# First loads on two queues, a reordered opening, and joined stores of tail rows in a fused attention and MLP kernel

## The chip, the cores and the metric

The kernel runs on one core of a Trainium2 chip. The time is the device time of one execution in microseconds (us). The core has a matrix engine (PE, with its weight loads PEld), a vector engine (DVE), a scalar engine (ACT), a general engine (POOL) and a queue engine (SP). SP, ACT and POOL can issue transfers ("SPq", "ACTq", "POOLq" in the profile); a column "DMA share" gives the mean busy share of the core's 16 transfer engines.

An execution over 1.5% above the fastest of the same kernel is marked slow and left out of the comparisons. The runs were made on several chips; each kernel is compared with the kernel before in the same rounds on the same chip. A profile is of one execution.

## The reference

```python
# attention: q, k, v of (8 batches, 8 heads, 576 tokens, 64), a band of 32 tokens to each side
scores = np.matmul(q, k.transpose(0, 1, 3, 2)) / np.sqrt(D)
scores = np.where(np.abs(pos[:, None] - pos[None, :]) <= 32, scores, -1e9)
x = softmax(scores) @ v                      # then (8 * 576, 512): tokens by heads and d
# MLP
h = x @ w_in                                 # 512 x 2048
g = 0.5 * h * (1 + np.tanh(c * (h + 0.044715 * h**3)))
out = g @ w_out                              # 2048 x 512
```

## The kernel before

The 4608 tokens are worked through in nine tiles of 512. While PE computes the MLP of tile t, the attention of batch t + 1 is slipped between its matmuls, by a fixed plan. In the opening, batch 0 has nothing to hide behind; `spin` issues matmuls without use, meant to keep PE's clock up. Queries are stored so that token 4p + j lies at (j, p), and the last 24 (in batch 0: 16) positions p, the "tail rows", are handled apart.

```python
def load_early(b):                      # opening: batches 0 and 1, all on SP
    def qk(h0):
        for src, dst in ((q, qr), (k, kr)):
            nc.sync.dma_start(dst[:, h0:h0 + 2, :], src[b, h0:h0 + 2, 0:512, :]...)
...
def load_v(b):                          # later batches: four casting loads on POOL, and the tail
    for c in range(4):
        nc.gpsimd.dma_start(V[:, c, :, :], v[b, :, 128 * c:128 * c + 128, :]...)
...
def cast_and_turn(b):                   # later batches: casts on DVE, transposes by transfers on SP
    ...
    nc.sync.dma_start_transpose(QTs[b]..., dst...)
    ...
            nc.sync.dma_start_transpose(KTs[b % 2]..., k16...)
...
def store(t, t4, yo, cols=slice(0, 512), eng=None):      # 128 rows of results
    m = 0
    while m < 128:
        ...                             # b, j, p of row m; n positions p to a j in this part
        e = min(n - p, 128 - m)
        ...
        (... nc.gpsimd).dma_start(out_v[b, j, q0 + p:q0 + p + e, cols], yo[m:m + e, cols])
        m += e
```

In the middle of the kernel POOL does, for each tile: eleven stores, then four V loads of a later batch. SP issues the transposes of the next batch's queries and keys (QT, KT).

The softmax here doesn't subtract the row's maximum and nothing guards it: scores larger than these inputs give would overflow.

## Time and profile before

| | before |
|---|---|
| median of the first 3 runs | 304.15 us (302.09 to 307.22) |
| span of the profiled run | 302.4 us, PE busy 96% |
| first product (x times w_in) starts | 21.03 us |
| second product (times w_out) starts | 40.86 us |
| from the first score of one middle batch to the next | 30.4 us |
| last result on DVE ready | 297.92 us |

The prediction shows the lines behind most of it. Three things that became important are not in it. The first is the transposes of a middle batch on SP's queue (start, length of the issue), which are issued in the first stretch of each tile:

```profile
94.67 3.44 SPq L324 DMA_TRANSPOSE QT<-q  x1
98.20 5.85 SPq L331 DMA_TRANSPOSE KT<-k  x2
```

The second is what POOL issues at that time: the stores of a tile, and right behind them the V loads.

```profile
91.75 7.10 POOL L515 DMA_DIRECT2D out_dram<-y  x11 [14.40 <-DVE y L580]
98.83 3.62 POOL L175 DMA_DIRECT2D V<-in_v_dram  x4
```

The first V load is issued 98.83 - 94.67 = 4.2 us after the QT transpose. The third is PE at the scores that need the transposes (start, length, what; idle time before and its cause would stand in brackets):

```profile
106.65 0.62 PE L360 MATMUL ps_s<-QT,KT 64*64 64x96 f16 x32
107.66 1.48 PE L551 MATMUL mm<-w_out,gT 128*128 128x256 f16 x12
...
110.92 0.40 PE L360 MATMUL ps_s<-QT,KT 64*64 64x96 f16 x16
```

No bracket: PE does not wait. The scores at 106.65 (head pairs 0 and 1) need the first of the two KT transposes, those at 110.92 (pair 2) the second. No view prints when these landed, but the trace holds the semaphore events: the first had landed at 105.68, so 1.0 us was to spare, and the second at 110.18. At batches 3 to 6 the spare time before the first scores was 1.0, 1.6, 3.6 and 1.6 us. The page did not show how little that was, since a wait that does not happen leaves no line.

### The profile page before, as it was taken

The numbers are of one execution on the slowest core, as the hardware profiler recorded it, in microseconds if no ns is written. First come the engines' busy times: TensorE is split into PE (matmuls) and PEld (weight loads), VectorE is DVE, ScalarE is ACT, GpSimd is POOL, SyncE is SP. The second block draws the span as 40 slices with busy tenths as digits, with TensorE's granted clock in tenths as the row PEclk, the third lists the DMA queues.
The fourth block names the chain that finished last, engine by engine and source line by source line (L and its number), as shares of the span: only waits on it lengthen the run. The fifth ranks groups of instructions, "written<-read, shape, count | busy, mean of one in ns | idle before, by whom it ended". The sixth has DMA issues, their size and how long they took to land.

```text
span 302.4 us, 7135 instructions
## 1 busy us (share of the span) xinstructions
PE 289.4 (96%) x2886; PEld 181.3 (60%) x2886; DVE 195.0 (64%) x429; ACT 186.9 (62%) x287; POOL 104.6 (35%) x160
## 2 busy tenths in 40 slices
PE   6869999999999999999999999999999999999993
PEld 2434545444785488547854785478547864784582
DVE  4682679969969566956685668566866635442442
ACT  1555767487856695669566956785668666606500
POOL 3555546357008500850085007600710070015000
PEclk9997999999999999999999999999999999999999
DMA  6989999999998999899979995999690031004013
GB/s 187 249 270 386 363 332 246 242 271 186 207 211 167 171 214 193 191 152 230 201 166 181 234 197 136 168 239 194 101 212 11 2 92 49 3 15 124 2 46 94
DMA packets 116831, 52.44 MB, mean 173 GB/s; under 512 B 97519, under 2 KB 109551, under 8 KB 116798
## 3 DMA queue, kind: packets, MB, share of 16 engines
q1 hardware_dynamic: 84233, 39.66, 59.7%
q0 software_dynamic: 31776, 11.41, 33.0%
q10 hardware_dynamic: 789, 0.92, 0.9%
q8 instruction: 22, 0.36, 0.5%
q14 instruction: 11, 0.09, 0.1%
HBM read 36.70 MB, written 9.44 MB: 153 GB/s over the span
## 4 chain that ended last, share of the span: by engine, by line
PE 71%; DMA 11%; SPq 8%; DVE 5%; POOL 2%; issue 2%; ACT 0%; DVEq 0%; POOLq 0%
PE mm L551 31%; PE mm L456 18%; PE ph L456 14%; DMA wst<-in_moe_w_in_dram 4%; DMA wst<-in_moe_w_out_dram 3%; SPq L145 3%; PE ps_s L360 2%; PE ps_d L389 2%; DMA kr<-in_k_dram 2%; DMA vr<-in_v_dram 2%; SPq L136 2%; DVE s L499 2%; PE ps_o L395 2%; SPq L167 2%; POOL w_in L201 1%
## 5 line engine op out<-in xcount | busy, mean ns | idle before, releaser
L456 PEld LDWEIGHTS <-w_in 128*128 128x128 f16 x576 | 56.4, 99 | 68.3 <-issue 2.4
L515 POOL DMA_DIRECT2D out_dram<-y x77 | 46.4, 611 | 113.0 <-DVE y L580 99.3
L456 PE MATMUL mm<-xT,w_in 128*128 128x512 f16 x320 | 79.3, 382 | 1.7 <-POOL w_in L201 1.7
L464 ACT ACTIVATE gT<-mm 128x512 f16<-128x512 f32 x80 | 47.6, 599 | 46.0 <-PE mm L456 45.2
L456 PE MATMUL ph<-xT,w_in 128*128 128x512 f16 x256 | 65.0, 383 | 0.0
L499 DVE TENSOR_TENSOR s<-gT 128x512 f16<-128x512 f16 x64 | 26.9, 420 | 41.7 <-ACT gT L464 41.7
L551 PEld LDWEIGHTS <-s 128*128 128x128 f16 x512 | 49.6, 98 | 5.9
L551 PE MATMUL mm<-t,s 128*128 128x256 f16 x376 | 44.7, 273 | 0.0
L370 ACT ACTIVATE pe<-ps_s 128x960 f16<-128x960 f32 (+1 forms) x32 | 30.5, 976 | 22.5 <-PE ps_s L360 22.4
L464 ACT ACTIVATE gT<-ph 128x512 f16<-128x512 f32 x64 | 36.0, 602 | 10.1 <-PE ph L456 9.9
L551 PEld LDWEIGHTS <-gT 128*128 128x128 f16 x384 | 36.0, 98 | 6.6
L551 PE MATMUL mm<-w_out,gT 128*128 128x256 f16 x256 | 32.8, 273 | 0.5 <-DVE y L562 0.5
L409 ACT ACTIVATE lt<-lt 128x480 f32<-128x480 f32 (+3 forms) x40 | 23.5, 587 | 1.3
L408 ACT ACTIVATE lt<-ps_d 128x480 f32<-128x480 f32 (+2 forms) x29 | 16.0, 553 | 11.1 <-PE ps_d L389 6.2
L175 POOL DMA_DIRECT2D V<-in_v_dram x24 | 22.0, 938 | 1.7 <-PE mm L456 1.3
L90 ACT ACT_TABLE_LOAD x17 | 21.8, 1283 | 1.1 <-PEq L812 0.8
L376 DVE TENSOR_TENSOR pe<-pe,band 128x960 f16<-128x960 f16 (+1 forms) x32 | 21.3, 684 | 1.0 <-ACT pe L370 1.0
L395 PEld LDWEIGHTS <-V 128*64 128x64 f16 x520 | 14.5, 111 | 4.0 <-DVE V L183 0.6
L551 PE MATMUL mm<-t,gT 128*128 128x256 f16 x128 | 16.3, 273 | 0.0
L418 DVE TENSOR_TENSOR xT<-ps_o,lt 128x480 f16<-128x480 f32 (+5 forms) x26 | 13.4, 535 | 2.0 <-ACT lt L409 1.9
L360 PEld LDWEIGHTS <-KT 64*64 64x64 f16 x576 | 9.6, 106 | 8.1 <-issue 5.8
L551 PE MATMUL mm<-w_out,s 128*128 128x256 f16 x120 | 14.4, 273 | 0.0
(90 smaller groups left out, 305.2 us busy)
## 6 DMA issues: line engine op xcount, KB each, us to landing
kr<-in_k_dram SPq DMA_DIRECT2D x32, 256.0 KB, 8.4
qr<-in_q_dram SPq DMA_DIRECT2D x6, 1024.0 KB, 7.8
wst<-in_moe_w_in_dram SPq DMA_DIRECT2D x3, 1024.0 KB
wst<-in_moe_w_out_dram SPq DMA_DIRECT2D x3, 1024.0 KB, 11.9
V<-in_v_dram POOLq DMA_DIRECT2D x24, 128.0 KB, 7.9
qr<-in_q_dram SPq DMA_DIRECT2D x8, 256.0 KB, 10.5
vr<-in_v_dram SPq DMA_DIRECT2D x16, 128.0 KB, 3.4
V<-V SPq DMA_DIRECT2D x5, 256.0 KB
```

Source lines behind the costliest of these rows:

```text
L90: nc.scalar.add_instruction(mybir.InstLoadActFuncSet(name=nc.get_next_instruction_name(), act_func_set_id=which, ins=[], outs=[]))
L175: nc.gpsimd.dma_start(V[:, c, :, :], v[b, :, 128 * c:128 * c + 128, :].rearrange("h p d -> p h d"))
L370: nc.scalar.activation(pe, ps[:, :, 0:w], AF.Exp, scale=SCALE)
L376: nc.vector.tensor_tensor(pe, pe, m.rearrange("k (o j) p -> k o j p", o=1).broadcast_to(list(pe.shape)), op=ALU.mult)
L395: nc.tensor.matmul(o[64 * h:64 * h + 64, cols].rearrange("d (j p) -> d j p", j=4)[:, :, p0 - q0:p1 - q0], Vs[b % 2][:, slot, 2 * pr + h, : ...
L408: nc.scalar.activation(lt[:, 0:n], d[:, 0:n], AF.Ln)
L409: nc.scalar.activation(lt[:, 0:n], lt[:, 0:n], AF.Exp, scale=-1.0)
L456: nc.tensor.matmul(ph, w_in16[:, dc, fc * 128:fc * 128 + 128], xT[:, dc, t * 512 % RING:t * 512 % RING + 512], start=(dc == 0), stop=(dc = ...
L464: nc.scalar.activation(gTs[t][:, fc, :], phs[fc], AF.Gelu_apprx_tanh)
L499: nc.vector.tensor_tensor(dst, x, y, op=op)
L515: (eng or turn_about[0] if t == NT - 1 else eng or nc.gpsimd).dma_start(out_v[b, j, q0 + p:q0 + p + e, cols], yo[m:m + e, cols])
L551: nc.tensor.matmul(pys["apart"][:, 0:256] if apart else py[:, blk, :], lhsT, wino[w][:, f, :], start=(new and i % (8 if one else 16) == 0) ...
```

## The change

It means to start the opening sooner: the first loads go out on two queues (SP and ACT), the ACT table load moves behind ACT's issues, w_in comes in halves, the attention of batch 0 is ordered anew with some copies on ACT and casts on DVE, and the first product runs chunk by chunk behind it. Besides, the stores of tail rows are joined: several blocks of j, each of 16 or 24 rows, in one transfer; and the last tile's stores are divided between SP and ACT in another way.

```diff
-            for src, dst in ((q, qr), (k, kr)):
-                nc.sync.dma_start(
+            for src, dst, eng in ((q, qr, nc.sync), (k, kr, nc.sync if b else nc.scalar)):
+                eng.dma_start(
...
+                eng = nc.scalar if not b and h in (1, 3) else nc.sync
...
-    load_table(exp_set)          (at the start)
+    load_table(exp_set)          (behind the first loads)
+    for i in range(4):
+        wi.append(load_w_in(i, stage_w(), 0, 2))
+        load_w_in(i, wi[i], 2, 4)
...
+            nj = 1 if p else max(1, min(4 - j, (128 - m) // n))
+            eng = engs[i % len(engs)] if engs else nc.gpsimd
+            if nj > 1:
+                e = nj * n
+                eng.dma_start(out_v[b, j:j + nj, q0:q0 + n, cols], yo[m:m + e, cols])
...                               (the opening: turns, casts, masks and weightings in a new order)
+    spread(0, 2, *ods[2])
+    spin(3, 512, 0)
+    for dc in range(3):
+        for fc in range(4):
+            ffn_in(0, fc, dc, dc + 1)
```

## The prediction

> **What bounds the kernel now.** I read the page first, then the matrix engine in order of time, then the waits, and last the transfers in short stretches. From the page (busy share of PE in 40 slices of 7.56 us, its granted clock, GB/s moved):
> ```profile
> PE 289.4 (96%) x2886; PEld 181.3 (60%) x2886; DVE 195.0 (64%) x429; ACT 186.9 (62%) x287; POOL 104.6 (35%) x160
> PE   6869999999999999999999999999999999999993
> PEclk9997999999999999999999999999999999999999
> ```
> PE is busy 96% of the span. It is not full in the first slices, in the last one, and in the fourth slice its clock falls. A change that removes no product work, as this one, can only gain there: at the opening and at the end. Much of the "busy" time of the opening is filler matmuls (spin). The matrix engine in order of time (start, length, what, idle time before):
> ```profile
> 21.03 0.39 PE L456 MATMUL mm<-xT,w_in 128*128 128x512 f16 x1 [1.52 <-POOL w_in L201]
> 21.59 0.39 PE L456 MATMUL mm<-xT,w_in 128*128 128x512 f16 x1 [0.17 <-POOL w_in L201]
> ...
> 40.86 0.38 PE L525 MATMUL mm<-w_out,gT 128*128 128x512 f16 x1 [0.29 <-POOL w_out L201]
> 41.61 1.67 PE L525 MATMUL mm<-w_out,gT 128*128 128x512 f16 x7 [0.37 <-POOL w_out L201]
> ```
> Twice PE waits for a weight cast: at the first product (21.03 us) and at the second product (40.86 us). From there on the idle times I could find are 0.33 us at 51.6, 0.41 at 60.4 and 0.54 at 79.8; 100 to 280 us is full. So the end moves by what the 40.86 point moves. What do the casts wait for? The waits of 20 to 60 us (total, times, longest):
> ```profile
> POOL w_in L201 <- DMA wst<-in_moe_w_in_dram: 6.6, 5, 1.9
> POOL w_out L201 <- DMA wst<-in_moe_w_out_dram: 6.2, 4, 2.9
> DVE w_in L201 <- DMA wst<-in_moe_w_in_dram: 5.7, 2, 4.1
> ```
> They wait for transfers, not for an engine. Until the second product starts, the kernel is bound by how soon the loads arrive. Short stretches of the opening (columns: busy us of PE, PEld, DVE, ACT, POOL; clock, DMA share, GB/s):
> ```profile
> 2.50:5.00 2.50, 2.50 (x10) 1.11 (x8) 1.34 (x7) 0.00 (x0) 0.50 (x2) 1.00 0.89 268
> ...
> 12.50:15.00 2.50, 2.18 (x41) 0.90 (x39) 2.46 (x5) 1.92 (x3) 1.74 (x3) 1.00 1.23 227
> 15.00:16.25 1.25, 1.25 (x22) 0.80 (x16) 1.16 (x3) 0.90 (x2) 0.69 (x2) 1.00 0.95 199
> 16.25:17.50 1.25, 1.00 (x22) 0.41 (x20) 1.22 (x3) 0.21 (x1) 0.63 (x2) 1.00 0.34 59
> ...
> 20.00:22.50 2.50, 1.30 (x21) 0.66 (x21) 1.67 (x4) 0.75 (x2) 1.90 (x4) 1.00 1.03 368
> 22.50:25.00 2.50, 2.50 (x12) 0.87 (x7) 0.69 (x1) 2.37 (x3) 0.76 (x2) 0.50 1.05 405
> ```
> Two things: a hole of 59 GB/s at 16.25 to 17.50, between the last values and the first weights, and PE at clock 0.50 in 22.5 to 25. The hole stands behind the one issuing queue:
> ```profile
> 7.29 2.05 SPq L136 DMA_DIRECT2D qr<-in_q_dram  x1
> ...
> 10.03 4.70 SPq L145 DMA_DIRECT2D vr<-in_v_dram  x6
> 14.77 3.97 SPq L192 DMA_DIRECT2D wst<-in_moe_w_in_dram  x5
> ```
> An undisturbed issue takes about 0.47 us; the twelfth took 2.05, and the first of w_in 1.57 (14.77 to 16.34). So the queue was held back, the weights were issued late, and the hole followed.
>
> **What the Trainium skill says.** "DMA: Bandwidth & Descriptors", section Issuing engines are not separate DMA queues, says that transfers issued from several engines run on the same 16 DMA engines and that this saves only the issuing time. The DMA share of 0.89 to 1.23 outside the hole agrees: there is little idle engine time to win. The same page, Why small descriptors are slow (HBM only), says that 256-byte rows lose part of the rate. The trace agrees: 199 to 227 GB/s while the values (64 floats, 256 B a row) come, 368 to 405 with weights. "TensorE: Matmul & The Clock Gate", Part 1, says that PE runs at half clock after about 3.4 us without work. Here the fall to 0.50 came after stretches with gaps of at most 1.52 us, so gaps shorter than that page's window count too. "ScalarE: Activation LUTs", What ACT_TABLE_LOAD costs, gives about 1283 ns; the trace shows 1283.
>
> **The change part by part.**
> *Two queues.* Seven of the opening loads (four k, the k tail, values of heads 1 and 3) move from SP to ACT. Batch 0 is q, k and v of 8x576x64 floats each, 3.54 MB; they are in at about 17.5 us (the stretches up to there sum to 3.6 MB). I see three gains. (a) The hole filled at 368 GB/s: (368-59)/368 x 1.25 = 1.05 us. (b) The slice 3.75 to 5.00 moves 162 GB/s, since the tails' issues take 0.62 to 0.75 us for 128 KB each; at the 301 of the next slice that is 174 KB more, 0.47 us at 368. (c) 10 to 16.25 us moves about 225 GB/s; if two queues raised it to the 277 of 5 to 7.5, 325 KB, 0.9 us; I count half, 0.45, for the share there is already over 1. Sum 2.0 us (estimate): all later loads of the queue come 2.0 us sooner.
> *Table load behind the issues.* Seven issues at about 0.6 us end near 5 us, the table load of 1.28 near 6.3; ACT's first work, a copy of QT, was ready on DVE at 5.72. Up to 0.6 us later for the first pair, not on the path: later pairs wait for data.
> *Weights in halves.* w_in 1 arrives whole at 24.7; in halves its first 512 KB (1.4 us at 368) is usable 1.4 us sooner. Casts split DVE/POOL: 0.43 us on DVE against 0.61 on POOL.
> *Attention reordered, product by chunk.* DVE takes two q casts (0.43 each), ACT two QT copies. The last group's weighting no longer stands behind the first two products (it ended at 22.5, though the last value cast ended at 18.4). With values in at about 16, weighting ends near 18, its two ACT steps (0.60 + 0.63) and the multiply (0.69) near 19.6. w_in 0 comes at 18.3 and 19.8, POOL casts by 21.0, PE starts at about 19 and runs 12 products. w_in 1 lands at 22.7: 14 more products, so the seventh column starts at about 25.2, against 28.9 before. PE is then 3.7 us earlier, data only 2.0. Spare PE speed is lost again in waits: w_in 2 (28.45 before) at 26.5, batch 1's k and q (32.7 to 36.5) at 30.7 to 34.5, w_out 0 (39.9) at 37.9. So the second product starts at about 38.9, not 40.86: **2.0 us**. This includes the cold clock: the eight slow products at 0.43 instead of 0.216 us cost 1.7, but w_out 0 would have been waited for anyway.
> *Stores.* At the end (timeline):
> ```profile
> 297.50 0.42 DVE L589 TENSOR_TENSOR y<-py,y 128x256 f32<-128x256 f32 x1 [0.45 <-PE py L551]
> 297.60 1.62 SPq L515 DMA_DIRECT2D out_dram<-y  x3
> 297.96 0.80 ACTq L515 DMA_DIRECT2D out_dram<-y  x2
> ```
> Results are complete at 297.92, but SP issues until 299.22, 0.85 us after what two fresh issues of 0.37 to 0.43 would need; the span ends at 302.4. The change cuts the last tile's issues from 22 to 16 (SP 11, ACT 5) and puts the last two on two queues, so the last issue should end near 298.35. I count **0.7 us**. The 18 joined issues on POOL, 0.61 us each, lie on an engine busy 35%: nothing.
> *Sum:* 2.0 + 0.7 = 2.7 us; 304.15 - 2.7 = 301.4.
>
> **The rivals.** *Transfers hidden or not sped up:* ACT's loads only interleave, and SP is again held at six values and the weights, so the hole stays. For it: the shared engines and shares near 1. Against: 1.4 of 3.5 MB leave SP's queue. Gain 0.5 + 0.7, time about 303. *Two queues overlap better than I think:* batch 0 at about 320 GB/s would be in at 13.6 us (2.5 + 11.1), some 3.9 us sooner: about 299.5. For it: the share reaches 1.36 at 60 to 100 us with several queues. Against: the page's rule, and the 256-byte rows. *PE bound instead of data:* the chunk order makes PE wait piece by piece, the clock halves again, and ACT, now issuing, copying and exponentiating, delays the attention. For it: four filler matmuls fewer around the scores. Against: 1.7 us of spare time between PE and data. Time 302 to 304. *Recovering the whole fall of the clock and the early start* would give 3.7 + 0.7, 299.8; the wait at 40.86 speaks against it.
>
> **Range and chances.** The gain runs from 0.5 to about 5 us by these; the three runs before spread from 302.09 to 307.22, so a median carries some 1.5 us of its own. Range 298.8 to 303.9. Faster by over 2% needs 298.1, more than any rival but the best with luck: 0.05. Slower by 2% would need a new wait of 6 us: 0.02. Within 2%: 0.93.
>
> **What would show it.** Right: no stretch under 150 GB/s between 3 and 20 us; last value cast near 16.5 instead of 18.4; w_out 0's first cast near 38 instead of 39.9; PE still waiting there for the cast; last SP issue under 0.6 us after the last DVE result. Wrong: the hole still there; a first product as early as said but w_out at 39.9 all the same; PE waiting for ACT or DVE and not for a cast; more clock lost than before; or PE waits of several tenths after 60 us that eat the gain.

## The result, and the profile after

The changed kernel takes 324.28 us in the median of 6 runs (323.63 to 326.89), the kernel before 303.92 (302.09 to 307.22) beside it: ratio 1.0707, 95% interval 1.0652 to 1.0763. All ratios here are the mean time of one kernel's fast runs over that of the other's of the same rounds, so not quite the ratio of the medians. The prediction was 301.4, with a range of 298.8 to 303.9. It missed by 23 us.

The page of the changed kernel (PE busy, its clock, in 40 slices of 8.05 us):

```profile
PE   5578999999999499994999899979999999999994
...
PEclk9579999999999979996899999998999999999999
```

Two things differ from before. The first slices are emptier, and in the middle there are new holes in PE's row (4, 4, 7) with a fall of the clock behind them. The waits say what PE lacked there (total, times, longest):

```profile
PE ps_s L359 <- DMA KT<-k: 11.9, 4, 4.5
```

Before, this line did not exist. PE in order of time at the first of these waits:

```profile
112.85 0.62 PE L359 MATMUL ps_s<-QT,KT 64*64 64x96 f16 x32 [4.25 <-DMA KT<-k]
113.86 2.70 PE L553 MATMUL mm<-w_out,gT 128*128 128x256 f16 x12
...
118.79 0.40 PE L359 MATMUL ps_s<-QT,KT 64*64 64x96 f16 x16
```

The scores waited 4.25 us for the transposed keys. Behind the wait, twelve matmuls took 2.70 us instead of 1.48: PE's clock had fallen to half. The next scores came 118.79 - 112.85 = 5.94 us later, before 110.92 - 106.65 = 4.27; so this wait cost 1.67 us more through the clock than it shows itself. (This agrees with the Trainium skill, "TensorE: Matmul & The Clock Gate", Part 1, which gives about 3.4 us without work for the fall; but at 216.3 the clock fell behind a wait of 2.25 us.)

SP's queue shows the transposes of that batch:

```profile
96.54 6.69 SPq L323 DMA_TRANSPOSE QT<-q  x1
103.33 7.44 SPq L330 DMA_TRANSPOSE KT<-k  x2
```

They start 1.9 us later than before, and their issues take 6.69 and 7.44 us instead of 3.44 and 5.85. On POOL, one store is now a joined one (L515), three issues are saved, and the V loads come 98.66 - 96.54 = 2.1 us after the QT transpose instead of 4.2:

```profile
93.63 2.33 POOL L517 DMA_DIRECT2D out_dram<-y  x4 [13.27 <-DVE y L582]
95.94 0.71 POOL L515 DMA_DIRECT2D out_dram<-y  x1
96.64 2.03 POOL L517 DMA_DIRECT2D out_dram<-y  x3
98.66 4.02 POOL L173 DMA_DIRECT2D V<-in_v_dram  x4
```

Over all batches, the list of transfers gives the median time from issue to landing, first of the kernel before, then of the changed one:

```profile
V<-in_v_dram POOLq DMA_DIRECT2D x24, 128.0 KB, 7.9
...
KT<-k SPq DMA_TRANSPOSE x12, 6.7
```

```profile
V<-in_v_dram POOLq DMA_DIRECT2D x24, 128.0 KB, 10.1
...
KT<-k SPq DMA_TRANSPOSE x12, 10.6
```

The V loads land 2.2 us later after their issue. The two numbers for KT are not of the same transposes: the list counts only transfers whose landing it can tell, here 2 and 3 of the 12. By the semaphore events of all 12 the median is 9.4 us against 7.4. And since the issues are slower too, more is lost on the way to the scores: from the start of the QT transpose to the landing of the first KT transpose it is 15.0 us instead of 10.0 (mean of batches 3 to 6). Those 5.0 us are more than the 1.0 to 3.6 us that were to spare. The work of the opening is the same in both kernels, and so is that of every tile. Where the time came in, by the starts of the scores of the middle batches:

| stretch | before | after | more |
|---|---|---|---|
| start to first score of batch 2 | 75.04 | 78.06 | 3.0 |
| to batch 3 | 31.61 | 34.79 | 3.2 |
| to batch 4 | 30.42 | 36.61 | 6.2 |
| to batch 5 | 30.42 | 34.00 | 3.6 |
| to batch 6 | 30.48 | 32.80 | 2.3 |
| to the start of the last DVE instruction | 99.53 | 101.10 | 1.6 |

So about 3 us appear up to batch 2 and 17 behind it. The opening itself went the other way from what was predicted. ACT in order of time:

```profile
0.81 0.52 ACTq L133 DMA_DIRECT2D kr<-in_k_dram  x1
...
7.08 0.37 ACTq L133 DMA_DIRECT2D kr<-in_k_dram  x1
8.76 0.38 ACTq L143 DMA_DIRECT2D vr<-in_v_dram  x1
9.16 1.28 ACT L90 ACT_TABLE_LOAD   x1 [9.16 <-DMA kr<-in_k_dram]
10.46 0.58 ACT L299 COPY QT<-pt 128x512 f16<-128x512 f16 x1
```

ACT's issues were held back like SP's, so its table load came at 9.16 us, the first QT copy behind it at 10.46, and the first scores at 11.82 instead of 7.74. The first product started at 28.22 instead of 21.03, the second at 44.98 instead of 40.86.

### The profile page after: what moved, and what is told of

It reads as the page before. It is cut to its first block, busy times and chain, and to the rows that moved or that the text cites. A ratio compares the mean times of both kernels' runs of the same rounds, so it can differ in the third digit from the quotient of the medians.

```text
span 322.1 us, 7109 instructions
## 1 busy us (share of the span) xinstructions
PE 294.8 (92%) x2884; PEld 184.3 (57%) x2884; DVE 193.2 (60%) x431; ACT 187.8 (58%) x289; POOL 92.9 (29%) x141
## 4 chain that ended last, share of the span: by engine, by line
PE 76%; DMA 15%; DVE 4%; ACT 2%; issue 1%; ACTq 1%; DVEq 0%
PE mm L553 31%; PE mm L455 15%; DMA KT<-k 13%; PE ph L455 13%; PE ps_s L359 4%; PE ps_d L388 3%; PE mm L527 2%; DMA kr<-in_k_dram 2%; PE ps_o L394 2%; PE py L527 2%; DVE KT L300 1%; PE ps_od L388 1%; PE spin L226 1%; PE ps_od L394 1%; ACT pe L369 1%
## 5 line engine op out<-in xcount | busy, mean ns | idle before, releaser
L455 PE MATMUL mm<-xT,w_in 128*128 128x512 f16 x320 | 78.2, 379 | 0.0
L517 POOL DMA_DIRECT2D out_dram<-y x55 | 32.9, 606 | 117.1 <-DVE y L582 103.4
L455 PE MATMUL ph<-xT,w_in 128*128 128x512 f16 x256 | 64.2, 379 | 0.0
L553 PE MATMUL mm<-t,s 128*128 128x256 f16 x376 | 45.8, 277 | 0.0
L553 PEld LDWEIGHTS <-gT 128*128 128x128 f16 x384 | 37.5, 102 | 8.1
L553 PE MATMUL mm<-w_out,gT 128*128 128x256 f16 x256 | 36.1, 291 | 0.0
L359 PE MATMUL ps_s<-QT,KT 64*64 64x128 f16 (+3 forms) x576 | 14.2, 228 | 17.2 <-DMA KT<-k 11.9
L359 PEld LDWEIGHTS <-KT 64*64 64x64 f16 x576 | 10.5, 113 | 25.2 <-DMA KT<-k 13.1
L173 POOL DMA_DIRECT2D V<-in_v_dram x24 | 23.1, 986 | 0.3 <-POOL after L728 0.3
L394 PEld LDWEIGHTS <-V 128*64 128x64 f16 x520 | 15.1, 115 | 5.4 <-DVE V L181 1.7
L564 DVE COPY y<-mm 128x512 f32<-128x512 f32 x8 | 5.5, 688 | 20.7 <-PE mm L553 20.7
L175 POOL DMA_DIRECT2D V<-in_v_dram x6 | 4.2, 697 | 45.2 <-PE ps_o L394 34.3
```

Of the source, the lines that this page charges most:

```text
L359: nc.tensor.matmul(ps[64 * half:64 * half + 64, h, 4 * n * r:4 * n * r + 4 * n].rearrange("k (j p) -> k j p", j=4)[:, :, p0 - q0:p1 - q0], ...
L394: nc.tensor.matmul(o[64 * h:64 * h + 64, cols].rearrange("d (j p) -> d j p", j=4)[:, :, p0 - q0:p1 - q0], Vs[b % 2][:, slot, 2 * pr + h, : ...
L455: nc.tensor.matmul(ph, w_in16[:, dc, fc * 128:fc * 128 + 128], xT[:, dc, t * 512 % RING:t * 512 % RING + 512], start=(dc == 0), stop=(dc = ...
L517: eng.dma_start(out_v[b, j, q0 + p:q0 + p + e, cols], yo[m:m + e, cols])
L553: nc.tensor.matmul(pys["apart"][:, 0:256] if apart else py[:, blk, :], lhsT, wino[w][:, f, :], start=(new and i % (8 if one else 16) == 0) ...
```

## The experiments

Fifteen kernels were run. Each gave the right result, but for the probe, which is wrong on purpose.

### a_rows_apart: the changed kernel without the joins

```diff
-            nj = 1 if p else max(1, min(4 - j, (128 - m) // n))
+            nj = 1
```

> The changed kernel with every store of the tail rows issued by itself again (one setting: the number of joined j is always 1); queues, weights, attention and the division of the last tile's stores as changed. Theory S (the joined stores, whose outer dimension is only 2 or 4, keep the transfers that feed the next batch's transposes waiting, which shows as PE waiting 4.25, 4.45 and 1.00 us for KT): these waits go, only the opening's loss of some 3 to 4 us stays, time 306 to 309. Theory O (the later opening alone shifts loads against products, and the waits follow from that): the waits stay, time 320 to 326.

Measured: 305.7 us (303.79 to 306.39), ratio 1.0066 (1.0008 to 1.0124). One setting takes away 18.6 us. No line "PE waits for KT" is left in its trace, and the distance of the scores is 30.4 us again. It is even a little under what was expected: in the profiled run (the fastest of the four) its second product starts at 42.67 us, 1.8 later than in before, but its last DVE instruction at 297.21, 0.3 sooner.

### b_join_only: the kernel before with the joins, nothing else

```diff
+            nj = 1 if p else max(1, min(4 - j, (128 - m) // n))
+            if nj > 1:
+                e = nj * n
+                use.dma_start(out_v[b, j:j + nj, q0:q0 + n, cols], yo[m:m + e, cols])
```

> The kernel before with nothing changed but the joined stores of tail rows. Theory S: PE waits for KT at the scores of the middle batches as in the changed kernel, 8 to 20 us in all, time 312 to 324, with an opening as before (second product at about 40.9 us). Theory O: 303 to 305, no waits for KT.

Measured: 322.67 us (321.75 to 323.28), ratio 1.0632 (1.0586 to 1.0679). The opening is that of before (second product at 40.02), and the wait is there:

```profile
PE ps_s L360 <- DMA KT<-k: 12.0, 4, 3.6
```

The waits follow the size of the join: tiles 1, 2 and 4 join four blocks in one store, and the scores of the batch behind wait 3.6 us each; tile 3 joins two, which also saves one issue instead of three, and the wait is 1.2 us.

So the joins alone are enough for nearly all of the loss, and theory O, by which the waits follow from the late opening, falls with both runs.

### c_one_queue: the changed kernel with one queue and the table load first

```diff
-            for src, dst, eng in ((q, qr, nc.sync), (k, kr, nc.sync if b else nc.scalar)):
+            for src, dst, eng in ((q, qr, nc.sync), (k, kr, nc.sync)):
...                               (the same for the k tail and values; the table load back at the start)
```

> The changed kernel with all first loads on SP again and the table load first. Theory Q (the opening lost because ACT's issues are held behind full queues until 9.1 us and its table load, the first QT copy and all scores wait behind them): ACT's table load at 0.8 us, first score near 8 us instead of 11.8, first product near 21 instead of 28.2, second product at 39 to 41 instead of 45.0; with theory S the waits for KT stay, time 314 to 321; with theory O the waits go too, time 300 to 305. If the reordered attention itself were at fault, the first product stays later than 25 us.

Measured: 322.5 us (318.59 to 322.96), ratio 1.0601. ACT loads its table at 0.81, and the second product starts at 41.05, as theory Q said; the waits for KT stay (13.3 us in all). But the first product starts at 24.29, 3.3 us later than in before, though the data come as in before: that part is the reordering itself. The time is no better than that of b or of the changed kernel: with the joins in, the opening no longer counts, since the transposes set the pace.

### d_two_queues_only: the kernel before with the two queues and the table load behind them

```diff
+            for src, dst, eng in ((q, qr, nc.sync), (k, kr, nc.sync if b else nc.scalar)):
...                               (also the k tail, the values of heads 1 and 3, and the table load)
```

> The kernel before with the first loads on two queues and the table load behind ACT's issues, nothing else. Theory Q: ACT is held as in the changed kernel, first exponential past 11 us instead of 8.4, second product at 41 to 45 us, time 304 to 308. My first reckoning (loads 2 us sooner, ACT free by 6.3): 302. Theory O: if the second product comes later by 3 us or more, waits for KT follow as in the changed kernel, and the time is 315 to 324.

Measured: 302.67 us (302.57 to 303.3), ratio 0.9983 (0.9937 to 1.0028). In the profiled run the second product starts at 39.26 us, 1.60 sooner than in the profile of before, and the last DVE instruction at 295.85, 1.65 sooner. That looks like the first reckoning (2.0), but it shows nothing: b_join_only, i_v_early, m_join_columns and o_join_pool_later have the opening of before unchanged, and in their profiles the second product starts at 40.02, 39.27, 38.72 and 38.71. ACT's table load comes at 8.19, and the first exponential right behind it at 9.49 instead of 8.44. By ratio the gain is not clear of noise either.

### e_join_pool_late: joined, but POOL no sooner at the V loads

A join saves up to three issues on POOL, and POOL then comes to the V loads sooner. Here copies without use fill the time that was saved.

```diff
+                if use is nc.gpsimd:
+                    for _ in range(nj - 1):
+                        nc.gpsimd.tensor_copy(filler, band[:, :, 0:128])
```

> The kernel before with joined stores, and behind each joined store as many copies on POOL (about 0.6 us each) as issues were saved, so that POOL comes to the V loads no sooner than before. Theory F (a joined store with an outer dimension of 4 or 2 is carried by only 4 or 2 of the 16 transfer engines, and what stands behind or beside it on those waits): the loss stays, 318 to 324. Theory P (fewer issues make POOL reach the V loads some 2 us sooner, and these then collide with the transposes): back to 303 to 306.

Measured: 305.21, 306.72, 311.44 and 314.1 us; the last two are marked slow, and the ratio of the two fast ones is 1.0076 (1.0003 to 1.0149). Theory F (318 to 324) is out, and the fast runs are near theory P (303 to 306): with POOL's time given back, most of the 19 us go although the joined stores are still there. The fast runs leave about 2.3 us. How much the joined stores cost here is less sure than the ratio says. The profiled run is one of the slow ones (314.1 us); it has 7.8 us of waits for KT, and two of its four stretches of half clock (at 108.8 and 143.0) stand right behind such waits. So it may be that these two runs are slow by the joins, and not by the state of the chip; that stays open.

### f_probe: the transfers by themselves

A kernel of transfers only, with a DVE instruction waiting behind each. Stores: one of 96 rows; four of 24 rows; one joined of 4 x 24 rows (192 KB in all three); then 48 rows and 2 x 24 joined (96 KB). Then two KT transposes, four V loads, or both, behind or beside such stores.

```python
def one(b):    nc.gpsimd.dma_start(o[b, 0, 0:96, :], y[0:96, :])
def apart(b):  # for j in range(4)
               nc.gpsimd.dma_start(o[b, j, 120:144, :], y[24 * j:24 * j + 24, :])
def joined(b): nc.gpsimd.dma_start(o[b, 0:4, 120:144, :], y[0:96, :])
```

> A probe that does no product work and gives a wrong result on purpose: single transfers one after the other, three times each. Theory F: 192 KB as one store of 96 rows land some 2 to 3 us after their issue at a DMA share that is high for a short time; the same as 4 x 24 rows joined at a share of about 0.25 while they run, some 2 us longer; 96 KB as 2 x 24 joined at about 0.125 and as long as the 192 KB; the four issues of 24 rows land each as fast as one store. Two transposes, or four V loads, with a joined store beside them land later than with the four apart, by some 1 to 3 us. Theory P: joined stores land no later than those apart, and transposes beside them neither.

In order of time, a single store of 96 rows and the joined one: start of the issue on POOL, and the DVE instruction that its landing released.

```profile
23.74 0.52 POOL L36 DMA_DIRECT2D out_dram<-y  x1 [4.61 <-DVE y L32]
26.45 0.48 DVE L32 MEMSET y<- 128x512 f32 x1 [1.94 <-DMA out_dram<-y]
...
31.67 0.71 POOL L43 DMA_DIRECT2D out_dram<-y  x1 [2.42 <-DVE y L32]
36.27 0.48 DVE L32 MEMSET y<- 128x512 f32 x1 [3.81 <-DMA out_dram<-y]
```

The single store lands 26.45 - 23.74 = 2.7 us after its issue began, the joined one 4.6, with the same bytes. The busy share of the 16 engines over each (columns: length, DVE and POOL busy, clock, DMA share, GB/s), for one store of 96 rows, for 4 x 24 joined, and for 2 x 24 joined:

```profile
24.30:26.45 2.15, 0.22 (x1) 0.00 (x0) 1.00 0.31 91
...
32.40:36.27 3.87, 0.06 (x2) 0.00 (x0) 1.00 0.19 51
...
40.90:44.83 3.93, 0.09 (x1) 0.00 (x0) 1.00 0.10 25
```

Half of the bytes as 2 x 24 rows take as long as 4 x 24 and half of the share. That they run on few engines is not shown by a view, but it fits what the Trainium skill says in "DMA: Bandwidth & Descriptors", section Why a DMA increments its semaphore by 16 and not by 1: the number of engines of a transfer divides the slowest dimension of both of its sides, so a side [4, 24, 512] allows 4 engines and [2, 24, 512] 2. By the profile the share stays at 0.19 and 0.10, under 4/16 and 2/16, with the latency in the stretch.

All of the probe, in us from the start of the first issue to the DVE instruction that waited (the range of three, or of the two or three clean ones):

| behind or beside | one store of 96 | four of 24 | 4 x 24 joined |
|---|---|---|---|
| the store itself | 2.7 to 2.8 | 3.7 | 4.6 to 5.0 |
| two KT transposes beside the store | 5.4 | 6.1 to 6.2 | 6.7 to 6.8 |
| the transposes, with four V loads behind the store | 9.6 to 10.2 | 8.1 to 8.3 | 11.0 to 12.2 |

The last row holds both causes. One plain store instead of four brings the V loads sooner, and the transposes beside them land some 1.5 to 2 us later (9.6 to 10.2 against 8.1 to 8.3). The joined store makes them later by some 1.5 us more. So both theories are right in the small, and neither alone. (A joined store without V loads delays the transposes by only 0.6 us against the four apart.)

### g_old_order: the changed kernel without joins and with the old order of the opening

> The changed kernel without the joins and with the attention and first products in the order of before (weights in halves, two queues, and the last tile's stores divided as changed are kept). If the reordering is what cost a_rows_apart 3 us against d_two_queues_only: second product near 39.3 us, time 301 to 303. If the halves of the weights or the stores' division are at fault: 304 to 306.

The edit puts the whole block from the first cast to the first products back as in before and sets nj = 1. Measured: 303.91 us (303.36 to 304.04), ratio 1.0005 (0.9961 to 1.0048). The second product starts at 40.29 (the first expectation said 39.3), and the profiled run has one wait of 0.6 us for KT. It is no slower than before and not clearly faster; d, on another chip, was at 302.67. So the time is 0.9 us above the one expectation (301 to 303) and under the other (304 to 306), and what remains lies within noise.

### h_act_freed: a_rows_apart, with ACT free

```diff
-    trans_out(0, 0, pt, nc.scalar.copy)
+    trans_out(0, 0, pt)
...                               (the table load back at the start)
```

> a_rows_apart with the table load first and the first QT copy on DVE again, so that ACT has nothing to do before the first exponential. If ACT's being held (table load at 7.8, first copy at 9.1 us) delays the opening of a_rows_apart: first score 1.5 to 2 us sooner, second product at 40 to 41 instead of 42.67, time 303 to 304. If the order itself does (first product behind the weighting of all four groups): second product above 42, time 305 to 306.

Measured: 303.24 us (302.52 to 304.23), ratio 0.9983. The first scores come at 9.15 instead of 10.46 us, but the second product at 42.16, only 0.5 us sooner. The first expectation was right in the time and wrong in the second product; the second the other way round. The time no longer goes with the start of the second product.

### i_v_early: V loads sooner, without any join

```diff
+            if 1 <= t <= 4 and q0 and j:
+                held.append((out_v[b, j, q0 + p:q0 + p + e, cols], yo[m:m + e, cols]))
...                               (issued in load_v, behind its four loads)
```

> The kernel before, no store joined; in tiles 1 to 4 the stores of tail rows other than the first block are put behind the next four V loads on POOL, so that these loads are issued up to three issues (about 1.8 us) sooner, as the joins do, but on stores that use the engines as before. Theory P (V loads issued sooner run into the transposes): PE waits for KT at the scores of the middle batches, time 308 to 318. If it is only the few engines (theory F): no waits, 303 to 305.

Measured: 305.22 us (302.97 to 306.54), ratio 1.0034 (0.9986 to 1.0082). In the profiled run (304.8 us of span, fast) the wait is there, shorter than with the joins:

```profile
PE ps_s L363 <- DMA KT<-k: 4.8, 3, 1.8
```

So sooner V loads do bring waits for KT, as theory P said, but theory P's 308 to 318 is wrong: with unjoined stores it costs 1 us or so, not clear of noise.

### j_best: the two queues with the last tile's stores divided

> d_two_queues_only with the last tile's stores divided between SP and ACT as changed (not joined): the parts of the change that help or do no harm. Second product near 39.3 us. From the last result on DVE to the end d took 4.6 us, a_rows_apart and g_old_order 4.3 to 4.4: 0.2 us less, time 302.0 to 302.8, 0.995 to 0.998 of before. My prediction's 0.7 us for the stores would give 301.9.

Measured: 303.02 us (301.99 to 304.28, 6 runs), ratio 0.9969 (0.9933 to 1.0004). From the last result on DVE (296.52 + 0.42) to the end of the span (301.9) it took 4.96 us, not less than before (4.48). Over the kernels with divided stores this last stretch is 4.0 to 5.0 us, over those without 4.3 to 4.6 (m_join_columns apart): no gain from the division is shown. This is the best version that the change holds, and it does not beat the kernel before clearly.

### k_halves: the two queues with w_in in halves

> d_two_queues_only with the w_in loads in eight halves. g_old_order (this and the divided last stores) began its second product at 40.29 us, d at 39.26, and took 303.9 against 302.7. If the halves do that: second product at 40 to 40.5 and 303.3 to 304.2. If not: 39.3 and 302.4 to 302.9.

Measured: 303.38 us (302.66 to 305.96, 6 runs), ratio 0.9991 (0.9952 to 1.003). The second product starts at 39.92; the halves cost at most some tenths, and gain nothing.

### l_reorder_one_queue: the reordered opening without queues and joins

> The changed kernel without the two queues and without the joins: the reordered attention, the product by chunks, halves, divided last stores. c_one_queue, the same with joins, began its first product at 24.3 and its second at 41.05 us. If that later opening counts only as far as the second product starts later than in before (40.86), nothing is lost: 303 to 304.5. If the first product's 3.3 us are on the path: 306 to 308.

Measured: 303.51 us (302.63 to 306.48), ratio 1.0002 (0.9953 to 1.0052). The first product starts at 24.51 instead of 21.03, the second at 41.28 instead of 40.86, and the last DVE instruction at 296.49. So 3.5 us at the first product, and 0.4 at the second, cost nothing at the end.

### m_join_columns: each joined store cut by columns

```diff
+                width = (cols.stop - cols.start) // nj
+                for c0 in range(cols.start, cols.stop, width):
+                    part = slice(c0, c0 + width)
+                    use.dma_start(out_v[b, j:j + nj, q0:q0 + n, part], yo[m:m + e, part])
```

> The kernel before with each joined store cut into as many column pieces as it joins blocks (4 x 24 rows x 128 columns, four times): as many issues on POOL as the rows apart, each again with an outer dimension of 4 or 2. The Trainium skill says that consecutive small transfers of POOL take their engines in turn. Theory F in the form that the load of one joined store on a few engines does it: spread over the pieces that load is gone, 303 to 306. If any transfer of this shape does harm, or it is more small packets: 308 to 322, KT waits as in e_join_pool_late or worse.

The expectation draws on the section of "DMA: Bandwidth & Descriptors" named at f_probe. Measured: 306.77 us (305.58 to 308.67), ratio 1.0084 (1.0008 to 1.016), with 3.3 us of waits for KT. It has the same shape of stores as b_join_only, in smaller pieces, and takes 16 us less. So the shape as such does not do it. Of what it loses, 1.8 us are not in the middle at all: in the profiled run it takes 6.3 us from the last result to the end of the span instead of 4.5, since the last tile's stores are cut into pieces too. Whether the pieces really run on different engines, no trace here shows. It has as many issues as the rows apart, and in that it is like e.

### n_join_one_tile: joins in one tile only

```diff
-            nj = 1 if p else max(...)
+            nj = 1 if p or t != 2 else max(...)
```

> The kernel before with joined stores in tile 2 only. If the loss is made afresh in every tile: the stretch from the scores after it is 4 to 5 us longer than 30.4, the later ones are 30.4 again, time 307 to 309. If one delay keeps the later batches late: all later stretches are long, 312 to 320. If a single tile's delay is taken up by the spare time of the transposes: 303 to 305.

Measured: 309.22 and 309.37 us fast, 314.49 slow, and one run of 422.78 at a clock of 0.66 throughout, which was the profiled one; its times are of no use. The ratio of the fast runs is 1.0181 (1.0085 to 1.0276): a single tile with joins costs about 5.5 us (1.8% of 304). That is the size of one long stretch in the table of the result. It fits a loss that is made afresh in each tile (of the four tiles whose stores stand before V loads, three join four blocks as this one does, and one joins two; the joins give 19 in all). The trace agrees, though PE runs too slowly in it to wait: from the start of the QT transpose to the landing of the first KT transpose it takes 15.1 us behind the joined tile, and 10.6, 8.4 and 10.3 us behind the others.

### o_join_pool_later: joined, with POOL later than before

```diff
-                    for _ in range(nj - 1):
+                    for _ in range(2 * nj):
```

> e_join_pool_late with more copies on POOL (two for each joined block, about 5 us behind 4 x 24 rows instead of 2.2), so that the V loads come later than in the kernel before. If the joined stores hurt only together with V loads beside the transposes: 303 to 305, steady, no KT waits. If the few engines hurt by themselves: 305 to 314 as e.

Measured: 304.6 us (303.14 to 306.21), ratio 1.0027 (0.9949 to 1.0105), with one wait of 2.7 us for KT in the profiled run. The stores are as joined as in b, and 18 us are gone. By time this is the first expectation; "no KT waits" was too much.

### What follows from b, e, i, m, n and o together

Two columns are read from the trace of each kernel's profiled run, both in us from the start of the QT transpose, mean of batches 3 to 6: when the first V load is issued, and when the first KT transpose has landed.

| kernel | stores joined | first V load | first KT landed | ratio to before |
|---|---|---|---|---|
| before | no | 4.1 | 10.0 | 1 |
| i_v_early | no | 2.1 | 12.5 | 1.0034 |
| e_join_pool_late | yes | 4.4 | 13.8 (slow run) | 1.0076 (2 of 4 runs) |
| o_join_pool_later | yes | 8.0 | 10.3 | 1.0027 |
| m_join_columns | yes, in pieces | 4.5 | 11.9 | 1.0084 |
| b_join_only | yes | 2.6 | 15.0 | 1.0632 |

(Seven other kernels have rows apart and V loads at 4.1 to 4.3; their KT lands at 9.5 to 10.5. The changed kernel and c_one_queue are like b: 2.6 and 2.7, then 15.0 and 15.3.)

By the fast runs, either alone costs less than 1%, both together 6.3%. The landing of KT does not jump like that: sooner V loads alone make it 2.4 us later, both together 5.0 us. What jumps is the cost. The first 1.0 to 3.6 us of a delay are spare and cost nothing; what is beyond them PE waits for, and behind the longer waits it runs at half clock as well. This is worked out from the traces; no run changes the spare time by itself. Joined stores with the V loads well behind them (o) make the landing hardly later on the mean, though one of its four batches waited 2.7 us.

## Why the prediction was wrong

**The step that failed** is the last sentence on stores: "The 18 joined issues on POOL, 0.61 us each, lie on an engine busy 35%: nothing." It counted an issue as POOL's time only. A join also changes the shape of the transfer and the time at which POOL reaches what stands behind it: the first KT transpose of a batch lands 5.0 us later, past its spare time, and PE waits. Measured by themselves, the joins cost 18.7 us (322.67 - 303.98 of the same rounds). No rival had it: all were about the opening and the end. (The count was off too: 7 stores on POOL are joined, in place of 22, which saves 15 issues.)

**What was in the profile and not read.** The prediction itself quotes a share of the transfer engines of 1.36 at 60 to 100 us with several queues, and it saw that PE was full from 100 to 280 us. It took a PE that does not wait for one that cannot be made to wait. The spare time of the first KT transposes was 1.0 to 3.6 us; no view gives it, and it takes the trace's semaphore events to see it.

**"Two queues", 2.0 us: not shown.** Half of it (1.05 us) was to come from filling the hole of 59 GB/s at 16.25 to 17.5 us. That hole is in the profile of before alone. b_join_only has the same opening on one queue, and moved 214 GB/s in that stretch (columns as in the prediction):

```profile
16.25:17.50 1.25, 1.00 (x23) 0.51 (x24) 1.22 (x3) 0.51 (x1) 1.06 (x2) 1.00 0.83 214
```

i_v_early, m_join_columns and o_join_pool_later, also with that opening, moved 237, 330 and 311 there, d_two_queues_only with two queues 199. Its second product was 1.60 us sooner than in the profile of before, but with the opening unchanged that start lies anywhere between 38.71 and 40.86. By time d's gain is 0.2%, and the interval (0.9937 to 1.0028) includes none.

**"Weights in halves": no gain.** Against d, k_halves took 0.9991 of the time of before instead of 0.9983, and its second product started no sooner (39.92 against 39.26).

**"Table load behind the issues": wrong.** Seven issues were to end near 5 us; the fourth k load was issued at 7.08, the table load ran at 9.16. The prediction had seen SP's queue held back, and did not expect it of ACT's. The changed order put a QT copy behind it: with ACT freed (h), the first scores came 1.3 us sooner than in a, the second product only 0.5. In the old order (d) the first exponential came 1 us later (9.49 instead of 8.44).

**"Attention reordered, product by chunk": wrong in the times, right that it is worth nothing by itself.** Weighting was to end near 18 and PE to start the product at about 19. With one queue the first product began at 24.3 and 24.5 (c, l), with two at 25.9 and 28.2 (a and the changed kernel, which have the same opening). The chain of copies, masks and value pairs on DVE, and the product behind the weighting of all four groups, take longer than the sum of two ACT steps and a multiply that was worked out.

**"So the end moves by what the 40.86 point moves": not so for a later start.** When the second product started 0.4, 1.3 or 1.8 us later (l, h, a), the last DVE instruction was 1.0, 0.3 and 0.3 us sooner. In d it started 1.6 us sooner, and so was the end; that is one profile. Between 40.86 and 60.39 the kernel before needs 19.5 us, a_rows_apart 18.4: with the later start the weights are there, and the short waits inside that stretch (0.7 us for w_out) go. A wait ahead of them only took their place.

**"Stores", 0.7 us at the end:** not there. The last issue ends 0.75 us after the last result in the changed kernel (318.53 against 317.78) and not 1.30 as in before, so the issues did become shorter. That is the joins' doing: with the old division and joins (b) it is 0.8 us, with the new division and rows apart (a, g, h) 1.8. But from the last result to the end of the span the trace has 4.3 us in the changed kernel and 4.5 in before, and 4.96 in j_best. What follows the last issue did not shrink with it: 3.6 us in the changed kernel, 3.2 in before.

**The clock.** The prediction had warned of new waits after 60 us and of more clock lost. That is what happened, by 12 us of waits and some 5 more behind them, where three stretches (13.6 us in all) ran at half clock, in tiles it had called full. It gave "slower by 2%" a chance of 0.02, and said what that would need: a new wait of 6 us.

**What stays open.** That joined stores and sooner V loads are both needed for the 19 us is shown by the fast runs of the table above; what the joined stores cost alone is not sure (e). That they are slow because they run on few engines is argued from the probe's shares and the skill's page, not shown. How they hold back the transposes, whether inside the transfer engines or in the issuing, no view here tells; and whether the columns of m run on more engines is not shown either.

## What to carry to other kernels

Before joining transfers to save issues, look at what the new outermost dimension is and how long such a transfer takes by itself: here 192 KB as 4 x 24 rows took 4.6 us, as four stores 3.7 and as one plain block 2.7. An engine that is busy 35% still sets when the transfers behind its issues start; look for what these will run beside, and for how much spare time the consumer of that has, even where it does not wait now. A loss that shows as a late opening is worth testing apart from one in the middle: both were there here, and only one counted. And before a gain is built on a feature of one profile, such as a hole in the transfers, look whether a second execution has it.

## What the Trainium skill lacked or had wrong

- "DMA: Bandwidth & Descriptors", Rules for kernel authors: "Coalesce into one large transfer" for many small ones. Joining four stores of 48 KB into one of 192 KB made it land 0.9 us later by itself (4.6 against 3.7 us) and the kernel 6% slower. The page's own rule on the slowest dimension (a dimension under 16 confines the transfer) fits the probe better (shares of 0.19 and 0.10 for 4 and 2 blocks).
- The same page does not say that an engine's issues can be held back, and with them the work behind them on that engine: behind seven issues ACT's table load came at 9.16 us. (Of what a second queue saves, no run here shows anything clear of noise: 0.9983, 0.9937 to 1.0028.)
- "TensorE: Matmul & The Clock Gate", Part 1: half clock after about 3.4 us without work. Waits of 4.25 and 4.45 us agree; but the clock also fell to half behind waits of 2.25 us (changed kernel, at 216.3) and 1.91 us (m_join_columns, at 108.3), and in the kernel before after gaps of at most 1.52 us.
- No page has that V loads issued 1.5 us sooner beside transposes make these land 1.5 to 2 us later (9.6 to 10.2 against 8.1 to 8.3 us in the probe; 12.5 against 10.0 in i_v_early, with V loads 2 us sooner).
